# An S5 state-space layer and a SwiGLU layer summed on one NeuronCore: rotations batched over pairs of quarters, and an order chosen among 72 plans

## The chip, the core and the metric

The kernel runs on one core of a Trainium2 chip. The metric is the device time of one execution in microseconds (us), as the median of several runs. The engines named below are PE (TensorE, matrix products and transposes into PSUM), DVE (VectorE), ACT (ScalarE), POOL (GpSimd) and SP (SyncE, here only a queue for DMA). Each engine works through its own list of instructions in order, and lists meet only at semaphores.

## What is computed

`x` has 2048 rows of 512. All of it is bf16 at the edges. With `xn` the layer norm of `x` over its 512 columns, the output is `x` plus an S5 layer of `xn` plus a SwiGLU layer of `xn`:

```python
Lam_bar = exp(dt * Lam)                        # 512 complex states
Bu = xn @ B_bar.T                              # complex
h[t] = Lam_bar * h[t-1] + Bu[t]                # over the 2048 rows
yA = 2 * real(h @ C.T) + xn * Dskip
yB = (silu(xn @ w_gate) * (xn @ w_up)) @ w_down   # 512 -> 1376 -> 512
out = x + yA + yB
```

## The kernel before, in words

The rows are cut into four blocks (b = 0 to 3) of 512 rows, each of four tiles of 128 rows. The hidden width 1376 is cut into 11 pieces (f = 0 to 10; the last has 96 columns). The 512 states are cut into four quarters q of 128, each with a real and an imaginary part c.

For each block the work is this, with lines of the kernel before:

- Layer norm statistics (L513, L515 on ACT, or L541, L556 on DVE), the normalised rows `xn` (L576 POOL, L579 and L584 ACT, L586 DVE), four transposes per tile into the PSUM tiles `pT` (L601, two of them in turn) and their copies into `xnT` (L606, L613 on ACT; L609, L614 on DVE). In block 0 the chain per tile is: statistics, a logarithm and an exponential on ACT (L545, L547), one small product on DVE (L549, called nmr below), then `xn` (even tiles on POOL, odd ones on ACT).
- Gate and up products: for each f, four matmuls `G_f` and four matmuls `U_f` over 512 rows (L780, in block 0 for f = 0 and 1 in pieces of 128 rows, L789), into four PSUM tiles `pA` used in turn. ACT takes `G_f` through SiLU (L799). In blocks 0 and 1 DVE multiplies the up product in PSUM with it (L807); in blocks 2 and 3 ACT copies it first (L802) and DVE multiplies in SBUF (L804). The product is `hT_f`.
- `S_in`: 8 groups of four matmuls (L755) make `Bu`, and ACT or DVE (L761, L762) copies each group to `U`.
- `ssm_chain`: a rotation by a table of cosines and sines turns the complex recurrence into two real ones. Per quarter: two products with the tables (L826 `ri_P`, L828 `ri_Q`), their sum (L830 `ri_V`), two scans with a real decay (L839), two products back (L842 `ro_P`, L844 `ro_Q`) and their difference (L846 `ro_H`), all on DVE. P, Q and V exist twice (`qs = q % 2`), so that two quarters can be under way at a time. The last column of each block, rotated (L853 to L859), starts the next.
- `DO`: per tile of 128 rows one PSUM tile `pACC` (two in turn) sums 8 matmuls of `H` with `CT` (L879), four with the diagonal of `Dskip` (L882) and 11 of `hT` with `wd` (L892). DVE adds `x` (L898, called final below), and SP stores the tile (L900).

Once only: transposes of B (L704, 4 sets of 8) with copies into `BT` (L708 DVE, L709 ACT); transposes of C (L722, 4 sets of 8, called CTr below), which ACT and DVE scale into `CT` (L729, L734 on ACT, L731, L736 on DVE); the tables (L678 to L691; the cosine table `c512` is the last one, L691 on ACT); and 12 matmuls on zeros at the start (L472).

The order of instructions is not that of the text. `add` records each operation with what it reads and writes, its engine (some may go to ACT or DVE, whichever is free) and an assumed duration, and `schedule` (L95) plans. `_backward` gives each operation a latest start from the planned PE order and a correction `boost`; this is its priority. `_forward` then simulates the engines: among the operations that are ready within `LOOK` = 450 ns the one of earliest priority goes next, and if that would leave a hole, a ready one that fits the hole goes before it. This is done three times. `emit` (L269) writes each engine's list with its waits. SP's DMAs all have one priority and go in the order of the text.

Of the kernel before, what the change touches and what calls it, by code (L numbers as in the profile page):

```python
# [2 lines left out]

# [10 lines left out]
_SYNC_LAT = 90.0  # L14
_DMA_LAT = 1900.0
_DMA_NS_PER_BYTE = 1.0 / 330.0
# [12 lines left out]
class _Prog:  # L29
# [65 lines left out]
    def schedule(self, iters=3):  # L95
        ops = self.ops
        n = len(ops)
        for op in ops:
            op.succ = []
        for op in ops:  # L100
            for d in op.deps | op.odeps:
                ops[d].succ.append(op.idx)
        t = self.pe_t0
        anchors = {}
        for op in ops:
            if op.eng == "pe":
                anchors[op.idx] = t
                t += op.dur
        for it in range(iters):
            self._backward(anchors)  # L110
            self._forward()
            prev = -1e15
            for op in ops:
                if op.eng == "pe":
                    v = op.start
                    if v < prev:
                        v = prev
                    anchors[op.idx] = v
                    prev = v
        return self.order  # L120

    def _backward(self, anchors):
        ops = self.ops
        n = len(ops)
        t_end = max(anchors[i] + ops[i].dur for i in anchors) + 3000.0
        big = 1e15
        ls = [None] * n
        nsucc = [len(op.succ) for op in ops]
        lf = [t_end] * n
        free_before = {}  # L130
        avail = []
        for op in ops:
            if nsucc[op.idx] == 0:
                avail.append(op.idx)
        placed = 0
        while avail:
            bi = 0
            bk = (lf[avail[0]], avail[0])
            for j in range(1, len(avail)):
                kk = (lf[avail[j]], avail[j])  # L140
                if kk > bk:
                    bk = kk
                    bi = j
            i = avail[bi]
            avail[bi] = avail[-1]
            avail.pop()
            op = ops[i]
            if i in anchors:
                s_ = anchors[i]
            else:  # L150
                e_ = min(lf[i], free_before.get(op.eng, big))
                occ = op.dur + (op.nbytes * _DMA_NS_PER_BYTE if op.dma else 0.0)
                s_ = e_ - occ
                free_before[op.eng] = s_
            ls[i] = s_
            placed += 1
            for d in op.deps | op.odeps:
                dop = ops[d]
                lat = 0.0 if d in op.odeps else _SYNC_LAT
                if dop.dma:  # L160
                    lat += _DMA_LAT
                v = s_ - lat
                if v < lf[d]:
                    lf[d] = v
                nsucc[d] -= 1
                if nsucc[d] == 0:
                    avail.append(d)
        assert placed == n
        for op in ops:
            if op.eng == "sp":  # L170
                op.prio = (0.0, op.idx)
            else:
                op.prio = (ls[op.idx] + op.boost, op.idx)

    def _forward(self):
        ops = self.ops
        n = len(ops)
# [6 lines left out]
        free_at = {e: 0.0 for e in engs}  # L184
        ready = {e: [] for e in engs}
        order = {e: [] for e in engs}
# [15 lines left out]
                push_ready(op.idx)  # L202
        dma_free = 0.0
        nsched = 0
        LOOK = 450.0

        def dur_on(i, e):
            o = ops[i]
# [2 lines left out]
        while nsched < n:  # L211
            best = None
            for e in engs:
                rl = ready[e]
                if not rl:
                    continue
                tmin = min(ops[i].ready for i in rl)
                t = max(free_at[e], tmin)
                cand = [i for i in rl if ops[i].ready <= t + LOOK]
                c = min(cand, key=lambda i: ops[i].prio)  # L220
                if ops[c].ready > t:
                    hole = ops[c].ready - t
                    fit = [i for i in rl if ops[i].ready <= t and dur_on(i, e) <= hole + 20.0]
                    if fit:
                        c = min(fit, key=lambda i: ops[i].prio)
                st = max(free_at[e], ops[c].ready)
                key = (st, st + dur_on(c, e))
                if best is None or key < best[0]:
                    best = (key, e, c)
            assert best is not None, "scheduler deadlock"  # L230
            (st, _k), e, c = best
            op = ops[c]
# [9 lines left out]
            if op.dma:  # L242
# [3 lines left out]
                else:  # L246
                    xs = max(issue_end, dma_free)
                    xe = xs + op.nbytes * _DMA_NS_PER_BYTE
                    dma_free = xe
# [6 lines left out]
            for s in op.succ:  # L256
                sop = ops[s]
                sop.nrem -= 1
                if c in sop.odeps:
                    r = (op.start + op.dur) if op.dma else op.end  # L260
                else:
                    r = op.end + _SYNC_LAT
# [66 lines left out]
def _d_dve(n, mode=1, naps=0, base=70.0):  # L329
    return base + 1.04 * n / mode + 60.0 * naps  # L330
# [7 lines left out]
def bass_parallel_sum__ssm_conv_s5__swiglu_ffn__prompt_kernel(  # L338
# [8 lines left out]
    add = pg.add  # L347
    add_flex = pg.add_flex

    with ExitStack() as es:  # L350
# [22 lines left out]
        hT = sb("hT", [128, 2, 11, 512], BF16)  # L373
        U = sb("U", [128, 2, 4, 2, 512], BF16)
        PQV = sb("PQV", [128, 3, 2, 2, 512], BF16)
        Pt = PQV[:, 0, :, :, :]
        Qt = PQV[:, 1, :, :, :]
        Vt = PQV[:, 2, :, :, :]
        G = sb("G", [128, 4, 2, 512], BF16)
        NH = 2  # L380
        H = sb("H", [128, NH, 4, 2, 512], BF16)
# [11 lines left out]
        YscK = [("H", 0, q) for q in range(4)]  # L393
        UscK = [("H", 1, q) for q in range(4)]
        RscK = [("G", q, c) for q in range(4) for c in range(2)]
        AscK = [("P", 0), ("P", 1), ("Q", 0), ("Q", 1)]
        c512 = sb("c512", [128, 4, 512], BF16)
        ssT = sb("ssT", [128, 4, 2, 512], BF16)
        NO = 3
# [12 lines left out]
        st = sb("st", [128, 8, 16], F32)  # L412
        pexp = sb("pexp", [128, 16], F32)
        init = sb("init", [128, 4, 2], F32)
# [56 lines left out]
        for w_ in range(NWARM):  # L471
# [8 lines left out]
            writes=["io_i"], dur=1000, name="iota")  # L480
# [329 lines left out]
        def ssm_chain(b, pr):  # L810
            rr, S5, C5 = pr["rr"], pr["S5"], pr["C5"]
            hb = b % NH
            ub = b % 2
            for q in range(4):
                qs = q % 2
                Uq = U[:, ub, q, :, :]
                Usw = bass.AP(U[:].tensor, Uq.offset + 512, [list(Uq.ap[0]), [-512, 2], [1, 512]])
                cc = c512[:, q, :].unsqueeze(1).to_broadcast([128, 2, 512])
                ss = ssT[:, q, :, :]
                Pq, Qq, Vq, Gq = Pt[:, qs, :, :], Qt[:, qs, :, :], Vt[:, qs, :, :], G[:, q, :, :]  # L820
                Gsw = bass.AP(G[:].tensor, Gq.offset + 512, [list(Gq.ap[0]), [-512, 2], [1, 512]])
                tabs = ["tab_s", "tab_ns", "tab_c"]
                uk = [("U", ub, q, 0), ("U", ub, q, 1)]
                gk = [("G", q, 0), ("G", q, 1)]
                d2 = _d_dve(1024, 2)
                add("dve", lambda e, Pq=Pq, Uq=Uq, cc=cc: e.tensor_tensor(Pq, Uq, cc, ALU.mult),  # L826
                    reads=uk + tabs, writes=[("P", qs)], dur=d2, name="ri_P")
                add("dve", lambda e, Qq=Qq, Usw=Usw, ss=ss: e.tensor_tensor(Qq, Usw, ss, ALU.mult),  # L828
                    reads=uk + tabs, writes=[("Q", qs)], dur=d2, name="ri_Q")
                add("dve", lambda e, Vq=Vq, Pq=Pq, Qq=Qq: e.tensor_tensor(Vq, Pq, Qq, ALU.add),  # L830
                    reads=[("P", qs), ("Q", qs)], writes=[("V", qs)], dur=d2, name="ri_V")
                for c in range(2):
                    if b == 0:
                        ini = 0.0
                        ir = []
                    else:
                        ini = init[:, q, c:c + 1]
                        ir = [("init", c)]
                    add("dve", lambda e, q=q, c=c, qs=qs, ini=ini: e.tensor_tensor_scan(  # L839
                            G[:, q, c, :], rr[0][:, q:q + 1].to_broadcast([128, 512]), Vt[:, qs, c, :], ini, ALU.mult, ALU.add),  # L840
                        reads=[("V", qs), rr[1]] + ir, writes=[("G", q, c)], dur=_d_dve(512, 0.5, 1, 75), name="scan")
                add("dve", lambda e, Pq=Pq, Gq=Gq, cc=cc: e.tensor_tensor(Pq, Gq, cc, ALU.mult),  # L842
                    reads=gk + tabs, writes=[("P", qs)], dur=d2, name="ro_P")
                add("dve", lambda e, Qq=Qq, Gsw=Gsw, ss=ss: e.tensor_tensor(Qq, Gsw, ss, ALU.mult),  # L844
                    reads=gk + tabs, writes=[("Q", qs)], dur=d2, name="ro_Q")
                add("dve", lambda e, q=q, Pq=Pq, Qq=Qq: e.tensor_tensor(H[:, hb, q, :, :], Pq, Qq, ALU.subtract),  # L846
                    reads=[("P", qs), ("Q", qs)], writes=[("H", hb, q)], dur=d2, name="ro_H")
            if b < NB - 1:
                a4 = G[:, :, 0, 511]
                b4 = G[:, :, 1, 511]  # L850
# [152 lines left out]
```

## Time and profile before

| What | us |
|---|---|
| median of 6 runs | 198.11 |
| lowest, highest run | 197.97, 198.95 |
| the profiled execution, its own time | 198.85 |
| its span, first to last instruction | 197.1 |
| time outside of the span (198.85 - 197.1) | 1.75 |
| PE busy | 188.3 |
| DVE busy | 161.3 |
| ACT busy | 93.2 |

The six runs were 198.18, 197.97, 198.04, 198.95, 198.75 and 197.99. A row of the timeline reads: start, duration, engine, line, operation, what it writes and reads, count, and in brackets the idle time before it with what ended it. The chain of waits, read in order of time, gives start, duration and line of the work that ended last, each step being what released the next.

### The profile page before, as it was taken

Reading aid. Unit: us, or ns where it says so; the run is one execution under the profiler, and the core shown is the slowest. Engines: PE = TensorE matmul, PEld = TensorE weight load, DVE = VectorE, ACT = ScalarE, POOL = GpSimd, SP = SyncE. Lnnn points to the kernel's source line nnn. Section 1 sums busy time; section 2 is a strip of 40 time slices with the busy share of each in tenths; the row PEclk is TensorE's granted clock in tenths of the full one; section 3 lists DMA queues with packets and bytes.
Section 4 is the critical chain, followed back from the end, with each engine's and each line's share of the span. In section 5 each row is a group of like instructions: output and inputs, shape, how many; then the busy total and the mean of one; then the engine's idle time right before and its main releaser. Section 6 shows DMA issues by size and latency. Waiting matters only on the chain.

```text
span 197.1 us, 2753 instructions
## 1 busy us (share of the span) xinstructions
PE 188.3 (96%) x1037; PEld 93.1 (47%) x1037; DVE 161.3 (82%) x306; ACT 93.2 (47%) x174; POOL 6.3 (3%) x13
## 2 busy tenths in 40 slices
PE   7698999979999979999999999999999999999993
PEld 2495444444455544454444454445444454444541
DVE  5779894679889999999999999989999999931111
ACT  3758586987777788550046643700266502100000
POOL 2300100020000000200000000000000000000000
PEclk9879999999999999999999999999999999999999
DMA  5999960000000000000000010000000000000110
GB/s 136 319 360 360 349 190 5 0 0 0 0 3 0 0 0 0 5 27 27 0 0 3 0 45 10 27 3 27 0 0 0 27 30 28 27 27 30 41 39 27
DMA packets 11197, 10.70 MB, mean 54 GB/s; under 512 B 592, under 2 KB 11184, under 8 KB 11184
## 3 DMA queue, kind: packets, MB, share of 16 engines
q1 hardware_dynamic: 11152, 10.52, 16.7%
q8 instruction: 8, 0.13, 0.3%
q14 instruction: 5, 0.04, 0.1%
q10 hardware_dynamic: 32, 0.00, 0.0%
HBM read 8.43 MB, written 2.10 MB: 53 GB/s over the span
## 4 chain that ended last, share of the span: by engine, by line
PE 87%; DVE 6%; ACT 2%; DMA 1%; issue 1%; POOL 0%; SPq 0%; DVEq 0%; ACTq 0%
PE pA L780 32%; PE pACC L892 19%; PE pA L755 14%; PE pACC L879 14%; PE pA L789 2%; PE pACC L882 2%; PE pT L601 2%; DMA xnat<-in_A_x_dram 1%; ACT xnT L613 1%; PE pT L722 1%; DVE bnst L541 1%; PE pT L704 1%; DVE ostage L898 1%; DVE PQV L826 1%; DVE PQV L844 1%; DVE PQV L828 1%
## 5 line engine op out<-in xcount | busy, mean ns | idle before, releaser
L799 ACT ACTIVATE sg<-pA 128x512 bf16<-128x512 f32 (+1 forms) x44 | 26.2, 596 | 52.1 <-PE pA L780 36.0
L780 PE MATMUL pA<-xnT,wu 128*128 128x512 bf16 (+1 forms) x168 | 43.1, 379 | 0.0
L780 PE MATMUL pA<-xnT,wg 128*128 128x512 bf16 (+1 forms) x168 | 43.1, 379 | 0.0
L892 PE MATMUL pACC<-wd,hT 128*128 128x512 bf16 (+1 forms) x176 | 40.6, 379 | 0.0
L879 PE MATMUL pACC<-CT,H 128*128 128x512 bf16 x128 | 30.3, 379 | 0.1
L755 PE MATMUL pA<-xnT,BT 128*128 128x512 bf16 x128 | 28.3, 379 | 1.7 <-ACT xnT L613 1.1
L839 DVE TENSOR_TENSOR_SCAN G<-sm,init,PQV 128x512 bf16<-128x512 f32 x24 | 29.9, 1273 | 0.0
L898 DVE TENSOR_TENSOR ostage<-pACC,xnat 128x512 bf16<-128x512 f32 x16 | 11.0, 688 | 19.2 <-PE pACC L892 19.1
L780 PEld LDWEIGHTS pA<-xnT,wg 128*128 128x128 bf16 (+1 forms) x168 | 16.7, 100 | 19.1
L780 PEld LDWEIGHTS pA<-xnT,wu 128*128 128x128 bf16 (+1 forms) x168 | 16.6, 100 | 18.7 <-DVE hT L807 0.4
L892 PEld LDWEIGHTS pACC<-wd,hT 128*128 128x128 bf16 (+1 forms) x176 | 16.5, 98 | 17.0
L755 PEld LDWEIGHTS pA<-xnT,BT 128*128 128x128 bf16 x128 | 12.4, 98 | 16.6 <-ACT xnT L613 2.0
L879 PEld LDWEIGHTS pACC<-CT,H 128*128 128x128 bf16 x128 | 12.4, 98 | 15.2 <-DVE ostage L898 0.2
L761 ACT ACTIVATE U<-pA 128x512 bf16<-128x512 f32 x25 | 14.7, 597 | 8.9 <-PE pA L755 8.7
L807 DVE TENSOR_TENSOR hT<-pA,sg 128x512 bf16<-128x512 f32 (+1 forms) x22 | 15.0, 686 | 4.4 <-PE pA L780 2.7
L802 ACT ACTIVATE su<-pA 128x512 bf16<-128x512 f32 (+1 forms) x22 | 13.1, 596 | 5.3 <-PE pA L780 5.3
L828 DVE TENSOR_TENSOR PQV<-U,ssT 128x1024 bf16<-128x1024 bf16 x16 | 11.0, 688 | 0.0
L826 DVE TENSOR_TENSOR PQV<-U,c 128x1024 bf16<-128x1024 bf16 x16 | 11.0, 687 | 0.0
L844 DVE TENSOR_TENSOR PQV<-G,ssT 128x1024 bf16<-128x1024 bf16 x16 | 11.0, 686 | 0.0
L842 DVE TENSOR_TENSOR PQV<-G,c 128x1024 bf16<-128x1024 bf16 x16 | 10.9, 681 | 0.0
L830 DVE TENSOR_TENSOR PQV<-PQV 128x1024 bf16<-128x1024 bf16 x16 | 10.7, 687 | 0.0
L846 DVE TENSOR_TENSOR H<-PQV 128x1024 bf16<-128x1024 bf16 x16 | 10.5, 686 | 0.0
(94 smaller groups left out, 159.1 us busy)
## 6 DMA issues: line engine op xcount, KB each, us to landing
out_dram<-ostage SPq DMA_DIRECT2D x16, 128.0 KB, 1.7
xnat<-in_A_x_dram SPq DMA_DIRECT2D x3, 512.0 KB, 9.3
wd<-in_B_w_down_dram SPq DMA_DIRECT2D x1, 1280.0 KB, 11.8
xnat<-in_A_x_dram SPq DMA_DIRECT2D x4, 128.0 KB, 2.4
wg<-in_B_w_gate_dram SPq DMA_DIRECT2D x1, 512.0 KB, 6.1
wu<-in_B_w_up_dram SPq DMA_DIRECT2D x1, 512.0 KB, 7.0
U<-in_A_B_re_dram SPq DMA_DIRECT2D x1, 512.0 KB, 8.0
U<-in_A_B_im_dram SPq DMA_DIRECT2D x1, 512.0 KB, 8.9
```

Source lines behind the costliest of these rows:

```text
L755: ins = e.matmul(pA[bank][:, :], BT[:, k, c * 512 + 128 * q:c * 512 + 128 * (q + 1)], xnT[:, b, k, :], start=(k == 0), stop=(k == 3))
L761: ("act", lambda e, q=q, c=c, bank=bank: e.activation(U[:, b % 2, q, c, :], pA[bank][:, :], AF.Copy), _d_act(512, True)),
L780: ins = e.matmul(pA[bank][0:fs, :], w[:, k, f0:f0 + fs], xnT[:, b, k, :], start=(k == 0), stop=(k == 3))
L799: add("act", lambda e: e.activation(sg[0:fs, slot, :], pA[bg][0:fs, :], AF.Silu), reads=[("pA", bg), "@t1"], writes=[("sg", slot)], dur=_d ...
L802: add("act", lambda e: e.activation(su[0:fs, slot, :], pA[bu][0:fs, :], AF.Copy), reads=[("pA", bu)], writes=[("su", slot)], dur=_d_act(51 ...
L807: add("dve", lambda e: e.tensor_tensor(hT[0:fs, b % 2, f, :], pA[bu][0:fs, :], sg[0:fs, slot, :], ALU.mult), reads=[("sg", slot)], writes= ...
L826: add("dve", lambda e, Pq=Pq, Uq=Uq, cc=cc: e.tensor_tensor(Pq, Uq, cc, ALU.mult), reads=uk + tabs, writes=[("P", qs)], dur=d2, name="ri_P")
L828: add("dve", lambda e, Qq=Qq, Usw=Usw, ss=ss: e.tensor_tensor(Qq, Usw, ss, ALU.mult), reads=uk + tabs, writes=[("Q", qs)], dur=d2, name="r ...
L839: add("dve", lambda e, q=q, c=c, qs=qs, ini=ini: e.tensor_tensor_scan(G[:, q, c, :], rr[0][:, q:q + 1].to_broadcast([128, 512]), Vt[:, qs, ...
L844: add("dve", lambda e, Qq=Qq, Gsw=Gsw, ss=ss: e.tensor_tensor(Qq, Gsw, ss, ALU.mult), reads=gk + tabs, writes=[("Q", qs)], dur=d2, name="r ...
L879: ins = e.matmul(pACC[bank][:, :], H[:, hb, q, c, tsl], CT[:, c * 4 + q, :], start=first, stop=False)
L892: ins = e.matmul(pACC[bank][:, :], hT[0:fs, hs, f, tsl], wd[0:fs, f, :], start=False, stop=(f == NF - 1))
```

## The change

Two things are changed. First, `ssm_chain` works on pairs of quarters: each of the six rotation operations covers 2048 elements per partition in place of 1024, and there is one P, one Q and one V in place of two half-sized ones. The 8 scans per block stay as they are. Second, `schedule` plans 72 times, over three values of the look-ahead (60, 250, 450), the hole rule on or off, random noise of several sizes on the priorities, and `boost` at full size or times 0.7. `_replay` walks each plan with exact durations and again with durations 6% longer (PE's excepted) and later releases; the plan with the least mean of the two is used. The one it settles on has a look-ahead of 60, the hole rule, noise of up to 200 with seed 2, and `boost` times 0.7. All other operations are those of before.

```diff
+        cands = []
+        for look in (60.0, 250.0, 450.0):
+            for hole in (True, False):
+                for sigma, seed in ((0.0, 0), (200.0, 1), (200.0, 2), (500.0, 3), (500.0, 4), (900.0, 5)):
+                    for bs in (1.0, 0.7):
+                        cands.append(dict(look=look, hole=hole, sigma=sigma, seed=seed, bscale=bs, iters=iters))
...
+        for p in cands:
+            self._sched_once(p)
+            nom = self._replay(1.0, 0.0)
+            pert = self._replay(1.06, 60.0)
+            score = 0.5 * nom + 0.5 * pert
...
+        self._sched_once(best[1])
...
+    def _sched_once(self, p):
...
+        rs = np.random.RandomState(p["seed"])
+        self._noise = rs.uniform(-1.0, 1.0, size=n) * p["sigma"]
+        self._bscale = p["bscale"]
+        self._look = p["look"]
+        self._hole = p["hole"]
...
+    def _replay(self, scale, lat_add):
...
+                    st = max(free_at[e], r)
+                    dur = op.dur * (scale if e != "pe" else 1.0)
...
-                op.prio = (ls[op.idx] + op.boost, op.idx)
+                op.prio = (ls[op.idx] + op.boost * self._bscale + self._noise[op.idx], op.idx)
...
-        LOOK = 450.0
+        LOOK = self._look
...
-                if ops[c].ready > t:
+                if self._hole and ops[c].ready > t:
...
-            for q in range(4):
-                qs = q % 2
...
-                d2 = _d_dve(1024, 2)
-                add("dve", lambda e, Pq=Pq, Uq=Uq, cc=cc: e.tensor_tensor(Pq, Uq, cc, ALU.mult),
-                    reads=uk + tabs, writes=[("P", qs)], dur=d2, name="ri_P")
...
+            d4 = _d_dve(2048, 2)
+            Pp, Qp, Vp = PQV[:, 0, :, :, :], PQV[:, 1, :, :, :], PQV[:, 2, :, :, :]
+            for pp in range(2):
+                q0 = 2 * pp
+                Up = U[:, ub, q0:q0 + 2, :, :]
+                Usw = bass.AP(U[:].tensor, Up.offset + 512, [pst, [1024, 2], [-512, 2], [1, 512]])
+                cc = c512[:, q0:q0 + 2, :].unsqueeze(2).to_broadcast([128, 2, 2, 512])
+                ss = ssT[:, q0:q0 + 2, :, :]
...
+                add("dve", lambda e, Up=Up, cc=cc: e.tensor_tensor(Pp, Up, cc, ALU.mult),
+                    reads=uk + tabs, writes=[("P",)], dur=d4, name="ri_P")
+                add("dve", lambda e, Usw=Usw, ss=ss: e.tensor_tensor(Qp, Usw, ss, ALU.mult),
+                    reads=uk + tabs, writes=[("Q",)], dur=d4, name="ri_Q")
+                add("dve", lambda e: e.tensor_tensor(Vp, Pp, Qp, ALU.add),
+                    reads=[("P",), ("Q",)], writes=[("V",)], dur=d4, name="ri_V")
...
+                add("dve", lambda e, Gp=Gp, cc=cc: e.tensor_tensor(Pp, Gp, cc, ALU.mult),
+                    reads=gk + tabs, writes=[("P",)], dur=d4, name="ro_P")
+                add("dve", lambda e, Gsw=Gsw, ss=ss: e.tensor_tensor(Qp, Gsw, ss, ALU.mult),
+                    reads=gk + tabs, writes=[("Q",)], dur=d4, name="ro_Q")
+                add("dve", lambda e, q0=q0: e.tensor_tensor(H[:, hb, q0:q0 + 2, :, :], Pp, Qp, ALU.subtract),
+                    reads=[("P",), ("Q",)], writes=[("H", hb, q0), ("H", hb, q0 + 1)], dur=d4, name="ro_H")
```

Built, the two kernels hold the same PE, ACT and SP work in other places, and DVE 48 rotation instructions in place of 96. Where PE's list is rearranged:

| Place | before | after |
|---|---|---|
| first gate and up pieces | transposes of tiles 0, 1, 2, then G and U in turn | transposes 0, 1, one G piece, transpose 2, three U pieces, ... |
| B transposes | one run of 32 between G_2 and U_2 | 16 after G_3 and G_2; U_2, U_3; then 16 |
| first C transposes | in block 1, after f = 4 | 8 of them between the row transposes of block 1 and its S_in |
| row transposes of block 2 | 8, U_10, 8 | U_10, then 16 |
| DO of block 0 | after G_0, U_0, G_1, U_1 of block 2 | after G_0 of block 2 |

On DVE and ACT the copies of `U` are shared differently, and DVE's chain of block 0 begins inside the first S_in. From G_2 of block 2 on PE's list is that of before.

More of the change, by code (lines that the diff above doesn't have):

```diff
@@ L1 @@
 import math
+import numpy as np
 from contextlib import ExitStack
@@ L102, in schedule @@
                 ops[d].succ.append(op.idx)
+        cands = []
[4 more added lines that the diff above has]
+                        cands.append(dict(look=look, hole=hole, sigma=sigma, seed=seed, bscale=bs, iters=iters))
+        best = None
+        self.trace = []
+        for p in cands:
[3 more added lines that the diff above has]
+            score = 0.5 * nom + 0.5 * pert
+            self.trace.append((score, nom, pert, p))
+            if best is None or score < best[0]:
+                best = (score, p)
+        self._sched_once(best[1])
+        self.best = best
+        return self.order
+    def _sched_once(self, p):
+        ops = self.ops
+        n = len(ops)
+        for op in ops:
+            if op.alts:
+                e0 = None
+                for e in op.alts:
+                    e0 = e
+                    break
+                op.eng = e0
+                op.fn, op.dur = op.alts[e0]
+        rs = np.random.RandomState(p["seed"])
[3 more added lines that the diff above has]
+        self._hole = p["hole"]
         t = self.pe_t0
@@ L108, in schedule @@
                 t += op.dur
-        for it in range(iters):
+        for it in range(p["iters"]):
             self._backward(anchors)
@@ L119, in schedule @@
                     prev = v
-        return self.order
+    def _replay(self, scale, lat_add):
+        ops = self.ops
+        order = self.order
+        ptr = {e: 0 for e in order}
+        free_at = {e: 0.0 for e in order}
+        end = {}
+        issue = {}
+        dma_free = 0.0
+        remaining = sum(len(v) for v in order.values())
+        mk = 0.0
+        while remaining:
+            progressed = False
+            for e, lst in order.items():
+                while ptr[e] < len(lst):
+                    i = lst[ptr[e]]
+                    op = ops[i]
+                    r = 0.0
+                    ok = True
+                    for d in op.deps:
+                        if d not in end:
+                            ok = False
+                            break
+                        v = end[d] + _SYNC_LAT + lat_add
+                        if v > r:
+                            r = v
+                    if ok:
+                        for d in op.odeps:
+                            if d not in end:
+                                ok = False
+                                break
+                            v = issue[d]
+                            if v > r:
+                                r = v
+                    if not ok:
+                        break
+                    st = max(free_at[e], r)
+                    dur = op.dur * (scale if e != "pe" else 1.0)
+                    if op.dma:
+                        ie = st + op.dur
+                        if op.nbytes < 65536:
+                            en = ie + op.nbytes * _DMA_NS_PER_BYTE + _DMA_LAT + 4 * lat_add
+                        else:
+                            xs = max(ie, dma_free)
+                            xe = xs + op.nbytes * _DMA_NS_PER_BYTE * scale
+                            dma_free = xe
+                            en = xe + _DMA_LAT + 4 * lat_add
+                        free_at[e] = ie
+                        issue[i] = ie
+                    else:
+                        en = st + dur
+                        free_at[e] = en
+                        issue[i] = en
+                    end[i] = en
+                    if en > mk:
+                        mk = en
+                    ptr[e] += 1
+                    remaining -= 1
+                    progressed = True
+            assert progressed, "replay deadlock"
+        return mk
@@ L375, in bass_parallel_sum__ssm_conv_s5__swiglu_ffn__prompt_kernel @@
         PQV = sb("PQV", [128, 3, 2, 2, 512], BF16)
-        Pt = PQV[:, 0, :, :, :]
-        Qt = PQV[:, 1, :, :, :]
-        Vt = PQV[:, 2, :, :, :]
         G = sb("G", [128, 4, 2, 512], BF16)
@@ L395, in bass_parallel_sum__ssm_conv_s5__swiglu_ffn__prompt_kernel @@
         RscK = [("G", q, c) for q in range(4) for c in range(2)]
-        AscK = [("P", 0), ("P", 1), ("Q", 0), ("Q", 1)]
+        AscK = [("P",), ("Q",)]
         c512 = sb("c512", [128, 4, 512], BF16)
@@ L813, in ssm_chain @@
             ub = b % 2
-            for q in range(4):
-                qs = q % 2
[L816 to L824, printed above, removed]
-                d2 = _d_dve(1024, 2)
-                add("dve", lambda e, Pq=Pq, Uq=Uq, cc=cc: e.tensor_tensor(Pq, Uq, cc, ALU.mult),
-                    reads=uk + tabs, writes=[("P", qs)], dur=d2, name="ri_P")
[L828 to L847, printed above, removed]
@@ new lines, in ssm_chain @@
+            pst = list(U[:].ap[0])
+            gst = list(G[:].ap[0])
+            tabs = ["tab_s", "tab_ns", "tab_c"]
+            d4 = _d_dve(2048, 2)
[6 more added lines that the diff above has]
+                ss = ssT[:, q0:q0 + 2, :, :]
+                Gp = G[:, q0:q0 + 2, :, :]
+                Gsw = bass.AP(G[:].tensor, Gp.offset + 512, [gst, [1024, 2], [-512, 2], [1, 512]])
+                uk = [("U", ub, q, c) for q in (q0, q0 + 1) for c in range(2)]
+                gk = [("G", q, c) for q in (q0, q0 + 1) for c in range(2)]
+                add("dve", lambda e, Up=Up, cc=cc: e.tensor_tensor(Pp, Up, cc, ALU.mult),
[4 more added lines that the diff above has]
+                    reads=[("P",), ("Q",)], writes=[("V",)], dur=d4, name="ri_V")
+                for qi in range(2):
+                    q = q0 + qi
+                    for c in range(2):
+                        if b == 0:
+                            ini = 0.0
+                            ir = []
+                        else:
+                            ini = init[:, q, c:c + 1]
+                            ir = [("init", c)]
+                        add("dve", lambda e, q=q, c=c, qi=qi, ini=ini: e.tensor_tensor_scan(
+                                G[:, q, c, :], rr[0][:, q:q + 1].to_broadcast([128, 512]), Vp[:, qi, c, :], ini, ALU.mult, ALU.add),
+                            reads=[("V",), rr[1]] + ir, writes=[("G", q, c)], dur=_d_dve(512, 0.5, 1, 75), name="scan")
+                add("dve", lambda e, Gp=Gp, cc=cc: e.tensor_tensor(Pp, Gp, cc, ALU.mult),
[4 more added lines that the diff above has]
+                    reads=[("P",), ("Q",)], writes=[("H", hb, q0), ("H", hb, q0 + 1)], dur=d4, name="ro_H")
```

## The prediction, as it was put on record

> **What bounds the kernel.** I read the engines' shares first, then PE's waits, then the chain of waits in order of time, and then timelines of the places that these name. The shares:
>
> ```profile
> PE 188.3 (96%) x1037; PEld 93.1 (47%) x1037; DVE 161.3 (82%) x306; ACT 93.2 (47%) x174; POOL 6.3 (3%) x13
> ```
>
> PE is busy for 188.3 of 197.1 us and the change leaves its matmuls alone, so only PE's holes and its slow stretches can be won. Four matmuls over 512 rows start every 0.8635 us (78.57, 79.44, 80.30, 81.16 in PE's timeline), a transpose every 0.055 us (0.44 for 8). PE's own waits, largest among them:
>
> ```profile
> PE pT L601 <- POOL xn L576: 1.1, 1, 1.1
> PE pA L755 <- ACT xnT L613: 1.1, 1, 1.1
> PE pA L755 <- DVE xnT L614: 0.6, 1, 0.6
> ```
>
> The first is the wait for the first normalised rows. The others, and one that is split over several rows, are places where PE transposes and then waits for the copies out of two PSUM tiles. The chain of waits shows three such places (start, duration, work):
>
> ```profile
> 15.08 0.91 PE pT L704 x16
> ...
> 16.01 1.03 ACT BT L709
> ...
> 17.09 0.62 PE pT L704 x8
> ...
> 39.41 0.46 PE pT L601 x8
> ...
> 41.04 0.44 DVE xnT L614
> ...
> 41.61 7.07 PE pA L755 x32
> ...
> 69.06 1.08 ACT xnT L613 x2
> ...
> 71.66 7.08 PE pA L755 x32
> ```
>
> From 71.66 to 194.02 the chain is PE without a hole worth naming. One more loss lies in the granted clock (columns: stretch, length, PE busy, clock, DMA):
>
> ```profile
> 5.00:8.50 3.50, 1.84 (x15) 1.00 1.03 301
> 8.50:12.00 3.50, 3.50 (x36) 0.51 1.08 374
> ```
>
> After 3.5 us with PE half idle, PE ran at half clock for 3.5 us.
>
> **Cost of the change on DVE.** 96 rotation instructions become 48. The rows say 687 ns each, but back to back they start 0.60 apart, since the end of one overlaps the next. Dependent neighbours do not overlap:
>
> ```profile
> 10.81 0.17 DVE L499 TENSOR_SCALAR sm<-sm 128x4 f32<-128x4 f32 x1
> 11.02 0.17 DVE L500 TENSOR_SCALAR sm<-sm 128x4 f32<-128x4 f32 x1
> ...
> 43.35 0.69 DVE L826 TENSOR_TENSOR PQV<-U,c 128x1024 bf16<-128x1024 bf16 x1
> 43.95 0.69 DVE L828 TENSOR_TENSOR PQV<-U,ssT 128x1024 bf16<-128x1024 bf16 x1
> ```
>
> [...] L499 to L500, where the second reads the first, start 0.21 apart, against 0.07 for independent small ones (112.77 and 112.84): a dependent neighbour costs 0.13. Before, two quarters alternated and hid this. In the built order of the new kernel six rotation steps directly follow what they read (0.13 each) and about eight have one tiny instruction between (0.06 each): 1.3 us. [...]
>
> **PE's places, one by one.** I walked the new lists of PE, ACT and DVE by hand, with durations of the rows (ACT copy 0.5 start to start, B copy 0.95, table step 1.8 to 2.0; DVE copy or hT from PSUM 0.60, scan 1.19).
>
> Head, +0.3. Tile 2's nmr, before at 6.3, now stands on DVE behind the parameter products and three L673, in the slot of tile 3's (8.23). POOL follows 0.35 later: `xn` of tile 2 at 9.3, transpose at 9.35 in place of 8.41. One G piece fills 0.43 of that; PE idles 0.5 more, and of this half is recovered because less work is left in the slow stretch. The G and U pieces end at about 14.37, not 14.05.
>
> B transposes, -0.87. Before: 14.91 to 17.54 for 32 x 0.055 = 1.76, so 0.87 lost on copies. Now G_3 and G_2 go first, the 16 transposes come at 16.1, U_2 and U_3 (1.73) cover two ACT copies (16.7 to 18.65), and the second 16 start at 18.7. U_5 then needs hT_3, which DVE reaches after the table step L683 and four L556 at about 21.4, against PE's arrival at 22.2: no wait. What if the cover is gone: up to 0.87 is back. U_10 ends at 31.75 (before 32.34).
>
> Between S_in of blocks 0 and 1, -0.07. Before 9.27 us from start to start; 6.91 are matmuls. Now the copies of the row transposes wait for DVE's second rotation and an ACT statistic, giving 9.2 us, but 8 C transposes (0.44) lie inside this hole and leave block 1.
>
> Block 1, -0.75. Before, from S_in to S_in 30.05 us. Now 6.91 + 22 x 0.8635 + 24 x 0.055 + 2.0 = 29.2; the 2.0 are 16 row transposes with their copies, now after U_10. Before the same piece, with U_10 inside it, took 2.86, that is 2.0 beside it: nothing is won there. The gain is the 0.44 moved and 0.23 of waits between C transposes, and about 0.1 of small ones. [...]
>
> DO of block 0, 0. It now starts one group after S_in, 7.8 us after that began. H must be ready: DVE's chain begins about 7.4 us earlier than before (the cosine table comes at 35.7, not 43.3, as ACT does it after one copy of `U`), carries six more copies of `U`, and ends 7.1 us after the start of S_in. Slack 0.7 us; before it was 0.3 (81.75 against 82.03).
>
> From there on the places are those of before, DVE is early, and the chain of block 3 is done some 12 us before its DO. Tail, stores and the 1.75 us outside the span are untouched. The new planner's search is done before launch and costs the chip nothing.
>
> Sum: +0.3 - 0.87 - 0.07 - 0.75 = -1.4 us. From the profiled 198.85 this gives 197.45; the median of 6 runs is 0.74 lower, so with the same difference 196.7.
>
> **Bounds.** Head: the late tile costs 0.2 to 0.6. [...] Taking the row's lesson that partly idle counts, the half clock could last one more window, in which PE does half the work: at most +1.7. At 16 to 18 the trace has 1.54 busy of 2 and keeps full clock, so I take 0, being nearer. The other waits: each of the four places can be wrong by about 0.3 either way; the largest gain, if all the holes named went, is 0.87 + 0.52 + 0.61 + 0.23 + 1.1 = 3.3, less the moved loads. The gain in an undisturbed clock is larger by up to 0.5, since PE then no longer stands before the B load.
>
> **Rivals.** (1) Hidden anyway: PE is at its floor and the new holes replace the old; then 198.1. For it: PE's 96%, and the late tile 2. Against: the holes at 15 and 57 have cover in the new order. (2) Half clock for a second window: -1.4 + 1.7 = +0.3, 198.4. It shares its result with (1). (3) Slower: DO of block 0 waits for H. If a dependent 2048-element operation waited longer than 0.13, the twelve rotations of block 0 would make H late, and every microsecond beyond the slack of 0.7 is PE idle, with nothing else in its list. [...] At 0.3 each it gives 3.6 - 0.7 - 1.4 = +1.5, 199.6. Against: dependent small ones lose 0.13, and fillers stand between most. [...]
>
> **How the numbers follow.** Forecast 0.70, its own range 195.8 to 197.5. Rivals (1) and (2) together 0.2, (3) 0.1. A difference of 0.3%, 0.6 us, is about what can be told from none. Faster: nearly all of the forecast and a little of the first rivals, 0.71; same 0.18; slower 0.11. The range is 195.7 to 198.3: it leaves out (3), and gains above 2.4.
>
> **What would show it.** Right: rotations of 2048 at 1.22 us, starting 1.13 apart; `xn` of tile 2 at 8.5 or later; B transposes in two runs of 16 with no hole between 16 and 23; S_in of block 1 at about 41, S_in of block 2 near 70.2 and DO of block 0 at 78, without a wait on H. Wrong: half clock after 12.5, a PE wait on L946, or hT waits in the first gate and up stage that eat the 0.87.

## The result, and the profile after

| What (us) | before | after |
|---|---|---|
| median | 198.21 (20 runs) | 196.16 (10 runs) |
| lowest, highest run | 197.75, 198.95 | 195.9, 198.0 |
| the profiled execution, its own time | 198.85 | 196.35 |
| its span | 197.1 | 194.6 |
| PE busy | 188.3 | 187.2 |
| DVE busy | 161.3 | 158.9 |

The ratio is 0.9923 with an interval of 0.9898 to 0.9948: faster by 0.5 to 1.0%, or about 1.5 us (2.05 by the medians). The forecast was 196.7. The page of the changed kernel, first the shares and then the costliest DVE group:

```profile
PE 187.2 (96%) x1037; PEld 91.7 (47%) x1037; DVE 158.9 (82%) x259; ACT 92.6 (48%) x173; POOL 7.3 (4%) x13
...
L924 DVE TENSOR_TENSOR PQV<-U,c 128x2048 bf16<-128x2048 bf16 x8 | 9.8, 1223 | 0.2
```

A rotation over 2048 elements takes 1.22 us. PE's waits after, without one of 1.2 on L567 at the start that both kernels have:

```profile
PE pT L696 <- POOL xn L671: 0.9, 2, 0.6
PE pA L850 <- DVE xnT L709: 0.6, 1, 0.6
PE pA L884 <- ACT xnT L701: 0.5, 1, 0.5
PE pT L696 <- ACT xnT L708: 0.5, 1, 0.5
```

The wait of 1.1 before S_in of block 2 (`pA` from the copy L613) is gone. In its place are two, 0.5 for a copy by ACT (L708) and 0.6 for one by DVE (L709), as all 16 row transposes now stand after U_10. The chain of waits in order of time (start, duration, work) shows what lies in the former holes:

```profile
9.20 0.40 PE pT L696 x4
...
13.17 1.73 PE pA L875 x8
14.89 0.89 PE pT L799 x16
15.79 1.73 PE pA L875 x8
17.51 0.89 PE pT L799 x16
18.41 12.18 PE pA L875 x56
...
38.68 0.61 ACT xnT L708
39.28 0.05 issue
39.33 0.62 PE pT L817 x8
39.95 6.95 PE pA L850 x32
...
68.80 0.44 DVE xnT L709
69.24 0.08 issue
69.32 7.07 PE pA L850 x32
76.38 0.86 PE pA L875 x4
77.25 1.73 PE pACC L979 x8
```

The two runs of B transposes (L799) stand between gate and up groups without a hole, eight C transposes (L817) stand ahead of the S_in of block 1, and DO of block 0 (L979) follows one group after the S_in of block 2, without a wait. A row of the chain starts when the work before it has ended; in PE's timeline a row starts when its first matmul does, some 0.17 earlier in a row without holes. So DO of block 0 is at 77.25 here and at 77.08 in the timeline. Places below are those of the timeline.

One caution on the pair of profiles. The profile before has the half-clock stretch at 8.5 to 12 us and the one after has not; here PE was busy for 2.67 of 3.5 us in the window ahead of it (stretch, length, PE busy, clock, DMA):

```profile
5.00:8.50 3.50, 2.67 (x17) 1.00 1.02 297
```

The order does not decide it alone. Of the 11 executions of the changed kernel, 7 ran at a mean granted clock of 0.997 or more (median 196.09) and 4 at 0.991 (median 197.77); the profile was one of the 7. The profile before, at 0.989, was the rarer case: of 41 later executions of that kernel, 6 were at 0.991 or less. For accounts I therefore use e5 and e6 below, both kernels at full clock throughout.

### The profile page after: what moved, and what is told of

Its sections match the earlier page's. It is cut to its first block, busy times and chain, and to the rows that moved or that the text cites. A ratio compares the mean times of both kernels' runs of the same rounds, so it can differ in the third digit from the quotient of the medians.

```text
span 194.6 us, 2700 instructions
## 1 busy us (share of the span) xinstructions
PE 187.2 (96%) x1037; PEld 91.7 (47%) x1037; DVE 158.9 (82%) x259; ACT 92.6 (48%) x173; POOL 7.3 (4%) x13
## 4 chain that ended last, share of the span: by engine, by line
PE 91%; DVE 4%; DMA 1%; ACT 1%; POOL 1%; issue 0%; SPq 0%; DVEq 0%
PE pA L875 37%; PE pACC L992 20%; PE pACC L979 14%; PE pA L850 13%; PE pACC L982 2%; PE pA L884 2%; PE pT L696 2%; DMA xnat<-in_A_x_dram 1%; PE pT L817 1%; DVE bnst L636 1%; PE pT L799 1%; POOL xn L671 1%; DVE U L857 1%; ACT xnT L708 1%; DVE PQV L926 1%; DVE PQV L924 0%
## 5 line engine op out<-in xcount | busy, mean ns | idle before, releaser
L875 PE MATMUL pA<-xnT,wu 128*128 128x512 bf16 (+1 forms) x168 | 42.5, 379 | 0.0
L875 PE MATMUL pA<-xnT,wg 128*128 128x512 bf16 (+1 forms) x168 | 42.5, 379 | 0.0
L979 PE MATMUL pACC<-CT,H 128*128 128x512 bf16 x128 | 30.2, 379 | 0.0
L939 DVE TENSOR_TENSOR_SCAN G<-sm,init,PQV 128x512 bf16<-128x512 f32 x24 | 29.4, 1271 | 0.0
L850 PE MATMUL pA<-xnT,BT 128*128 128x512 bf16 x128 | 28.3, 379 | 0.6 <-DVE xnT L709 0.6
L850 PEld LDWEIGHTS pA<-xnT,BT 128*128 128x128 bf16 x128 | 12.4, 98 | 15.4 <-DVE xnT L709 0.7
L979 PEld LDWEIGHTS pACC<-CT,H 128*128 128x128 bf16 x128 | 12.5, 98 | 14.9
L856 ACT ACTIVATE U<-pA 128x512 bf16<-128x512 f32 x23 | 13.7, 596 | 8.8 <-PE pA L850 8.7
L924 DVE TENSOR_TENSOR PQV<-U,c 128x2048 bf16<-128x2048 bf16 x8 | 9.8, 1223 | 0.2
L946 DVE TENSOR_TENSOR H<-PQV 128x2048 bf16<-128x2048 bf16 x8 | 9.8, 1222 | 0.0
L942 DVE TENSOR_TENSOR PQV<-G,c 128x2048 bf16<-128x2048 bf16 x8 | 9.8, 1221 | 0.0
L944 DVE TENSOR_TENSOR PQV<-G,ssT 128x2048 bf16<-128x2048 bf16 x8 | 9.8, 1220 | 0.0
L928 DVE TENSOR_TENSOR PQV<-PQV 128x2048 bf16<-128x2048 bf16 x8 | 9.8, 1220 | 0.0
L926 DVE TENSOR_TENSOR PQV<-U,ssT 128x2048 bf16<-128x2048 bf16 x8 | 9.8, 1219 | 0.0
```

Source lines behind the costliest of these rows:

```text
L850: ins = e.matmul(pA[bank][:, :], BT[:, k, c * 512 + 128 * q:c * 512 + 128 * (q + 1)], xnT[:, b, k, :], start=(k == 0), stop=(k == 3))
L856: ("act", lambda e, q=q, c=c, bank=bank: e.activation(U[:, b % 2, q, c, :], pA[bank][:, :], AF.Copy), _d_act(512, True)),
L875: ins = e.matmul(pA[bank][0:fs, :], w[:, k, f0:f0 + fs], xnT[:, b, k, :], start=(k == 0), stop=(k == 3))
L924: add("dve", lambda e, Up=Up, cc=cc: e.tensor_tensor(Pp, Up, cc, ALU.mult), reads=uk + tabs, writes=[("P",)], dur=d4, name="ri_P")
L926: add("dve", lambda e, Usw=Usw, ss=ss: e.tensor_tensor(Qp, Usw, ss, ALU.mult), reads=uk + tabs, writes=[("Q",)], dur=d4, name="ri_Q")
L939: add("dve", lambda e, q=q, c=c, qi=qi, ini=ini: e.tensor_tensor_scan(G[:, q, c, :], rr[0][:, q:q + 1].to_broadcast([128, 512]), Vp[:, qi, ...
```

## The experiments

Each starts from one of the two kernels. `place(eng, op, after)` moves one operation in an engine's finished list. The intervals of the ratios are against the kernel before.

**e1 and e2: each half of the change alone.** e1 is the `ssm_chain` of before under the new `schedule`; e2 is the new `ssm_chain` under the old `schedule`.

```diff
 e1
-    def schedule(self): (one plan)
+    def schedule(self): (72 plans, _sched_once, _replay)
 e2
-            for q in range(4):            (96 rotations)
+            for pp in range(2):           (48 rotations)
```

> The rotations of before (96 of 1024), planned with the new search, which here settles on noise of up to 500 with seed 4. Theory (the order of PE's list makes the gain): as the changed kernel or nearly, ratio to before 0.990 to 0.995, since this list too splits the B transposes and puts 8 C transposes before the second S_in. Rival (the time that the paired rotations take from DVE makes it): 1.00, 198.2 us.

> The paired rotations with the planner of before (look-ahead 450, no noise). Its list keeps the B transposes in one run of 32. Theory (order): ratio 0.997 to 1.003, the B transposes lose about 0.85 us as before. Rival (DVE's saving): 0.990 to 0.995, about 196.5 us.

e1: 196.81, ratio 0.9925 (0.9913 to 0.9938). e2: 203.33, ratio 1.0243 (1.0225 to 1.0261). The search alone gives most of the gain, although it settles on another plan (noise up to 500, look-ahead 60). At full clock e1 has 196.80 and the kernel before, in the same set of runs, 198.29: 1.5 us, where e3 below, with the order of the changed kernel, has 2.2 (196.05). What is missing lies in the head: S_in of block 0 starts at 31.03, in e3 at 30.24, and PE waits 1.0 for the load of B. Pairing alone costs 5 us, which no theory had. PE's waits in e2 are headed by this row:

```profile
PE pT L598 <- DVE CT L733: 1.9, 1, 1.9
```

and DVE's timeline there shows what PE waits behind:

```profile
68.06 1.22 DVE L826 TENSOR_TENSOR PQV<-U,c 128x2048 bf16<-128x2048 bf16 x1
69.20 1.22 DVE L828 TENSOR_TENSOR PQV<-U,ssT 128x2048 bf16<-128x2048 bf16 x1
70.33 0.74 DVE L733 SCALAR_TENSOR_TENSOR CT<-pT,sm,ctmp 128x512 bf16<-128x512 bf16 x1
```

The last scaling of C (L733) reads one of the two `pT` tiles, and the row transposes of block 2 need that tile. The old planner puts two rotations, now 2.26 us in one piece, ahead of it. What follows is in the windows (stretch, length, busy and count of PE, PEld, DVE, ACT and POOL, then clock, DMA, GB/s):

```profile
66.00:74.00 8.00, 4.01 (x28) 2.12 (x28) 8.00 (x10) 6.74 (x17) 0.00 (x0) 0.85 0.00 0
74.00:78.00 4.00, 4.00 (x10) 1.44 (x10) 4.00 (x6) 1.19 (x2) 0.00 (x0) 0.50 0.00 0
```

PE is idle for half of 8 us, and then runs at half clock. From the S_in of block 1 to that of block 2 e2 takes 33.49 us, the kernel before 30.05, and the S_in of block 2 itself takes 8.9 in place of 6.9. Two of the five executions of e2 had the clock of this profile (0.982; 203.60 and 203.74), three a higher one (0.992; 202.66 to 203.33).

**e3 and e9: the order held, the rotations cut.** e3 keeps every list of the changed kernel and issues each of the six rotations as two of 1024 elements (e9: as four of 512).

```diff
-  e.tensor_tensor(Pp, Up, cc, ALU.mult)
+  for h in range(2):
+      ins = e.tensor_tensor(Pp[:, h, :, :], Up[:, h, :, :], cc[:, h, :, :], ALU.mult)
```

> The changed kernel with every list in its order, but each paired rotation issued as two of 1024 elements one after the other: DVE does 48 more instructions, some 3.2 us. Theory (order): the time of the changed kernel within 0.3 us, as PE has 0.84 us in hand at the DO of block 0 (H ends at 76.24, DO starts at 77.08) and 12 more issues cost 0.8. Rival (DVE's saving): 2 to 3 us slower than the changed kernel, the time of before.

> The changed kernel with every list in its order, but each paired rotation issued as four of 512 elements: DVE gets 144 more instructions, some 9.6 us, of which 12 x 3 x 0.067 = 2.4 us lie before H of block 0 is done. Theory (PE's slack at that DO is 0.84 us and nothing else in PE's list covers it): DO of block 0 waits about 1.5 us, and the later hT and finals add little; 197 to 199 us. Rival (DVE is far from PE's path everywhere): 196.1.

Both expectations take 0.067 us for an added instruction, an estimate. By starts, a rotation of 2048 elements takes 1.13 in one piece (after, 86.55 to 87.68), 1.21 in two (e3, 72.34 to 73.55) and 1.35 in four (e9, 74.43 to 75.78): 0.07 to 0.08 for each added instruction.

e3: 196.06, ratio 0.9898 (0.987 to 0.9926), that of the changed kernel (0.9923). With the order fixed, the fewer instructions are worth nothing that can be measured. e9: 200.62, ratio 1.0143 (1.0098 to 1.0187), above the 197 to 199 of the theory. DVE does begin to bind when it gets more fixed cost, but not where I had said. DO of block 0 starts at 78.90 and `H` is done at 78.67: still 0.23 to spare. PE waits at the row transposes and the end tiles instead:

```profile
PE pT L696 <- DVE xnT L709: 2.2, 2, 1.6
PE pACC L985 <- DVE ostage L1004: 1.8, 1, 1.8
```

The wait of 1.6 ends at 118.45, ahead of the S_in of block 3, and the one of 1.8 at 170.80, at an end tile. From the S_in of block 1 to the end of `H` e9 took 37.0 us, the changed kernel 36.43. DVE was busy for 36.76 and 35.27 of these, so it did 1.49 more in 0.57 more time: its own waits took up most of the load. The profiled execution of e9 (202.26) had the half clock as well. In it a first window with 2.40 of 3.5 us busy was followed by half clock, and its first B transpose came 1.64 later than in e3, whose lists are the same. The other three executions ran at 0.997 or more and took 200.54 to 200.63, so the 4.5 us that the median lies above the changed kernel are not clock.

**e4: the B transposes in one run again.** The changed kernel, with all 32 after G_3 and G_2, and U_2 and U_3 behind them.

```diff
+  place("pe", find("pe", "BTr", 2), find("pe", "BTr", 1))
+  place("pe", find("pe", "BTr", 3), find("pe", "BTr", 2))
```

> The changed kernel with PE's list altered in one place: the 32 B transposes in one run after G_3 and G_2, U_2 and U_3 after them. Theory (order, with cover of the copies by U_2 and U_3 worth 0.87): 0.8 to 0.9 us slower than the changed kernel, with PE waits on the B copies of that sum. Rival (the clock alone makes the difference of the two kernels): no difference beyond noise.

197.31, ratio 0.9975 (0.9951 to 1.0). Among executions at a clock of 0.997 or more it is 197.27 against 196.09: +1.2, where 0.8 to 0.9 was expected. S_in of block 0 starts at 31.59, not 30.43. PE's waits name the copies, and PE's timeline shows where:

```profile
PE pT L799 <- ACT BT L804: 1.0, 2, 0.7
...
14.35 1.05 PE L799 MATMUL pT<-ident,U 128*128 128x128 bf16 x16
16.10 0.62 PE L799 MATMUL pT<-ident,U 128*128 128x128 bf16 x8 [0.70 <-ACT BT L804]
17.01 0.62 PE L799 MATMUL pT<-ident,U 128*128 128x128 bf16 x8 [0.30 <-ACT BT L804]
17.47 1.89 PE L875 MATMUL pA<-xnT,wu 128*128 128x512 bf16 x8
```

The waits of 1.0 count from the end of the last matmul; in a row without holes the next one starts some 0.17 before that end. By starts, the 32 transposes take 3.12 us (14.35 to 17.47) for 1.76 of work: 1.36 lost. Before it was 0.87. There DVE made the first copy that PE waits for (0.69 us); here ACT makes both (1.02 each). S_in of block 0 comes 1.35 later than in e3, and 0.12 of it comes back before the S_in of block 1. So this one cover, taken out of the new order, costs more than half of the gain.

**e5 and e6: both kernels at full clock.** A few matmuls on zeros (6 in e5, 8 in e6) go into early holes of PE; their results are not used.

```diff
+  def warm(i, n): op i also issues n matmuls on zeros into pACC[1]
+  warm(last, 4); warm(tt_[1], 2)
+  warm(pe[nm.index("Gt")], 2)        (e6 only)
```

> The kernel before with six more matmuls on zeros, four after the last one at the start and two after the second row transposes, so that PE has no hole of half a microsecond between 6 and 8.5; their result is not used. Theory (the half clock at 8.5 to 12 comes from those holes and costs this kernel little, since PE then waits for the B load): no run with a granted clock under 0.997, time 198.0 to 198.4, ratio 0.997 to 1.000. Rival (the half clock is most of what separates the two kernels): 197 or less.

> The changed kernel with eight more matmuls on zeros in its three holes between 6 and 9.2 (four, two, two); their result is not used. Theory: the runs near 197.5 to 198.0 with clock 0.991 disappear and all are at 195.9 to 196.4. Rival (clock drops come whatever PE does): the share of such runs stays at a third.

e5: 197.97, ratio 0.999 (0.9976 to 1.0004). e6: 196.12, ratio 0.9896 (0.9883 to 0.9909). None of their 16 executions had a clock below 0.998, where the changed kernel had 4 of 11 at 0.991. The kernel before gains little by it, for two reasons. Its median of 198.13 in the same set of runs is already one of full clock (15 of 17 executions; the two others took 198.77 and 199.06). And this row appears among PE's waits in e5:

```profile
PE pT L704 <- DMA U<-in_A_B_im_dram: 0.5, 1, 0.5
```

PE arrives earlier and stands before the load of B. The half clock delayed the first B transpose by only 0.97 (13.94 in e5, 14.91 in the profile before). The changed kernel has one more group ahead of the B transposes and reaches them at 14.53 (e6), without such a wait, so it loses more by the half clock: 1.7 (197.77 against 196.09). With the clock out of the way the two differ by 1.85.

**e7 and e8: the late tile 2 mended.** e7 is the changed kernel with the exponentials and nmr products of tiles 2 and 3 moved ahead of what the search had put before them. e8 adds six of the matmuls on zeros.

```diff
+  place("act", find("act", "ln_exp", 2), find("act", "ln_ln", 2))
+  place("act", find("act", "ln_exp", 3), find("act", "ln_ln", 3))
+  place("dve", n3, n2); place("dve", n2, find("dve", "prm32", 0))
```

> The changed kernel with two places of the head altered: on ACT the exponential of tiles 2 and 3 right after their logarithm, on DVE the small product of tile 2 right after the copy of the parameters and that of tile 3 in its old slot. Theory (the late tile 2 costs the head 0.3): third row transposes at about 8.3 instead of 9.2, PE's wait of 0.57 there gone, 0.3 to 0.5 us faster than the changed kernel. Rival (the head waits for something else anyway): no change.

> Both alterations, with six matmuls on zeros (four, two). Theory: sum of the two, 195.6 to 195.9 with no run of low clock, faster than both kernels. Rival: the zeros delay the rows that matter and eat the gain, 196.1.

e7: 195.88, ratio 0.9886 (0.9872 to 0.9899). e8: 195.68, ratio 0.9878 (0.9863 to 0.9892), the best of all. The third transposes come at 8.14 in place of 9.20, but a new wait of 0.28 for a copy (L704) follows, and S_in of block 0 starts 0.4 to 0.6 earlier (29.81 against 30.23 in e6 and 30.43). In time it is 0.2 (195.88 against 196.09) to 0.4 (195.68 against 196.12), less than the 0.3 to 0.5 expected of e7; the intervals of e6, e7 and e8 overlap, so the size is not firm.

**e10: the loss of e2 mended.** e2 with the last C scaling ahead of the two rotations on DVE, and the last two row-transpose copies ahead of five statistics on ACT.

```diff
+  before("dve", cw, hm)
+  before("act", tev[2], st1)
+  before("act", tev[3], st1)
```

> The paired rotations in the old planner's order (203.3 us), with two things moved: on DVE the last scaling of C goes ahead of the two rotations that stand before it, on ACT the last two copies of the row transposes of block 2 go ahead of five statistics. Theory (that paired rotation, 2.26 us in one piece, holds the PSUM tile that the row transposes need, and the hole of some 4 us behind it costs PE its clock for 3.4 us more): the hole and the half clock go, S_in of block 2 takes 6.9 us, 4 to 5.5 us faster, 198 to 199.5. Rival (pairing costs DVE time that shows elsewhere): 201 or more.

200.95, ratio 1.0136 (1.0108 to 1.0164). By the ratios, 2.1 of e2's 4.8 us come back; the theory had 4 to 5.5, and the result lies almost at the rival's 201. The half-clock stretch is gone (clock 1.00 from 60 to 80) and the S_in of block 2 is 31.05 after that of block 1. Two new waits take part of it:

```profile
PE pACC L881 <- DVE H L848: 0.8, 1, 0.8
PE pA L752 <- DVE hT L804: 0.7, 1, 0.7
```

The first is the prediction's third rival, at its place, in an order that leaves `H` no slack. DVE's total load does not explain it: it is busy for 157.5 us here and 161.3 before. Against e5, PE ends 3.4 us later in this profile: 0.7 before the S_in of block 0 (PE waits 1.2 for the load of B, in e5 0.5), 1.0 between the S_in of blocks 1 and 2, and 2.0 after that, where the two rows lie; 0.3 is gained between the S_in of blocks 0 and 1. So the two places named for e2 are about half of what pairing costs in the old order. Of the rest, 1.5 is PE waiting for DVE in the two rows.

## Why the prediction was right

The theory was that the gain lies in PE's order and not in DVE's lighter load. e1 and e3 show this, and e4 shows which piece of the order holds most of it. The number itself was met with some luck, as the last points show. The starts of S_in at full clock, in e5 (L755) and e6 (L850):

```profile
31.37 7.07 PE L755 MATMUL pA<-xnT,BT 128*128 128x512 bf16 x32
40.63 7.07 PE L755 MATMUL pA<-xnT,BT 128*128 128x512 bf16 x32 [0.61 <-DVE xnT L614]
70.68 7.08 PE L755 MATMUL pA<-xnT,BT 128*128 128x512 bf16 x32 [1.05 <-ACT xnT L613]
119.35 7.07 PE L755 MATMUL pA<-xnT,BT 128*128 128x512 bf16 x32
...
30.23 7.07 PE L850 MATMUL pA<-xnT,BT 128*128 128x512 bf16 x32
39.61 7.08 PE L850 MATMUL pA<-xnT,BT 128*128 128x512 bf16 x32
69.11 7.07 PE L850 MATMUL pA<-xnT,BT 128*128 128x512 bf16 x32 [0.56 <-DVE xnT L709]
117.55 7.07 PE L850 MATMUL pA<-xnT,BT 128*128 128x512 bf16 x32
```

The time between them, in us:

| Piece | e5 (before) | e6 (after) | difference | predicted |
|---|---|---|---|---|
| start to S_in of block 0 | 31.37 | 30.23 | -1.14 | +0.3 - 0.87 = -0.57 |
| S_in of block 0 to block 1 | 9.26 | 9.38 | +0.12 | -0.07 |
| block 1 to block 2 | 30.05 | 29.50 | -0.55 | -0.75 |
| block 2 to block 3 | 48.67 | 48.44 | -0.23 | 0 |
| S_in of block 3 to the end of PE | 73.68 | 73.67 | 0 | 0 |
| sum | | | -1.80 | -1.4 |

- **Head, +0.3.** Tile 2's transposes came at 9.20 (predicted 9.35). Mending the lateness is worth 0.2 to 0.4 (e7, e8), about the size predicted.
- **B transposes, -0.87.** From the first of them to S_in is 17.43 in e5 with 17 groups behind them. Less one group of 0.8635 that is 16.57, and e6 takes 15.70: -0.87 as predicted. Taking the cover away costs 1.2 rather than "up to 0.87" (e4), since PE then waits for two copies by ACT. With the head's +0.3 that makes -0.57; the table has 0.57 more, about as much as e5's hole before the load of B: 0.46 in the row of waits, 0.62 by starts. The prediction named this as a possible gain in an undisturbed clock, outside of its sum.
- **Between S_in of blocks 0 and 1, -0.07.** It was +0.12: the eight C transposes lie in the hole, after an ACT copy at 38.68, and the hole is a little longer than I had walked.
- **Block 1, -0.75.** It was -0.55. (The prediction's own 30.05 and 29.2 would give -0.85; the -0.75 is its list of gains, 0.44, 0.23 and 0.1.) The step that was off is "the 2.0 are 16 row transposes with their copies". By starts they took from 67.06 to 69.32 after, 2.26 us, with waits of 0.47 for ACT and 0.56 for DVE. In part this was misread before: the 2.86 came from the chain, whose row starts at 68.80, but PE's timeline has

```profile
68.64 0.61 PE L601 MATMUL pT<-ident,xn 128*128 128x128 bf16 x8
```

  and so 3.02 to the S_in at 71.66, 2.16 without U_10. With 2.16 the working gives -0.66. The row transposes became 0.1 longer instead of staying as they were, and that is the rest.
- **DO of block 0, 0, with a slack of 0.7.** `H` ended at 76.24 and DO began at 77.08: slack 0.84 and no wait. That rotations of 2048 elements would start 1.13 apart was an estimate that no row of before shows; it held after. The rival's price was also near: dependent rotations start 1.26 apart, independent ones 1.13 to 1.14, so a dependent neighbour costs 0.13, as taken from the small operations. DVE's and PE's timelines after:

```profile
75.02 1.22 DVE L946 TENSOR_TENSOR H<-PQV 128x2048 bf16<-128x2048 bf16 x1
77.08 1.89 PE L979 MATMUL pACC<-CT,H 128*128 128x512 bf16 x8
...
87.68 1.22 DVE L944 TENSOR_TENSOR PQV<-G,ssT 128x2048 bf16<-128x2048 bf16 x1
88.94 1.23 DVE L946 TENSOR_TENSOR H<-PQV 128x2048 bf16<-128x2048 bf16 x1
```

- **DVE.** Busy time fell by 2.4 (161.3 to 158.9), beside PE's work. In it are two more copies of `U` on DVE (9 in place of 7, and ACT 23 in place of 25) and one `xn` fewer, 0.9 us at the paces of the rows; so the rotations saved about 3.3, an estimate. At the 0.07 to 0.08 an instruction of e3 and e9, 48 fewer make 3.4 to 3.8. e9 shows where this cost binds: at the row transposes (a wait of 1.6) and end tiles (1.8), and not at DO of block 0, as the third rival had it.
- **"From there on the places are those of before", 0.** It was -0.23. Before, the DO of block 1 waited 0.2 for a final (L898): from the row transposes ahead of it 0.66 by starts (114.88 to 115.54), in e6 0.45. This wait is gone, and I had not listed it.
- **The clock.** I took a second half-clock window as the risk, and none was seen. What I missed is that the first one need not occur: at a given order it comes in some executions only (4 of 11 after). The prediction carried the profile's stretch over to both kernels. On that premise S_in of block 0 would start some 1.65 later than in e6 (e9 against e3 shows 1.64), at 31.9 against 32.34 before, which is -0.44 where -0.57 was predicted. The rows below it stay as in the table, and the sum is -1.1, not -1.4. The medians of the executions with the stretch agree roughly: 197.77 after, 198.6 to 198.9 before. In the other 7 of 11 executions the change is worth about 2 (1.8 in the table), in part since PE then no longer stands before the B load. The step from 197.45 to 196.7 has the same flaw. The 0.74 between the profiled execution and the median was carried over as a fixed difference, but it is probably for the most part what the half clock costs the kernel before (0.3 in the set run with e1, 0.8 in the one with e5), and the same stretch costs the changed kernel 1.7. So the predicted 196.7 is met partly by luck, because the two errors have opposite signs: the terms were 0.3 too favourable, and the clock was better than assumed.

What stays open: what decides in which executions the half clock comes, and what costs e10 the 1.0 between the S_in of blocks 1 and 2. Putting U_10 back between the two halves of block 2's row transposes was not tried in the new order.

## What to carry to other kernels

When one engine is busy for 96% and the edit lightens another, price the order and not the load: list the bounded engine's holes one by one and ask which work the new order puts into each. Longer pieces on a helper engine save fixed cost (here 0.07 to 0.08 us an instruction) but delay the small hand-offs behind them (in e2 PE waited 1.9 us for one), and an order planned for short pieces can lose far more than the saving (5 us here). Before comparing two profiles, look whether the granted clock was the same in both, and in how many executions.

## What was not expected of the hardware

- **The half clock came after windows that were only partly idle, and their idle share did not foretell it.** In the first window, PE busy for 1.84 (before) and 2.40 (e9) of 3.5 us was followed by half clock; 2.67 (after), 3.13 (e5) and 3.34 (e8) kept full clock. But so did 2.05 (e7) and 2.08 (e10), and the least busy one of all, that of e1 (stretch, length, PE busy, clock, DMA):

```profile
5.00:8.50 3.50, 1.54 (x16) 1.00 1.04 309
8.50:12.00 3.50, 3.50 (x66) 1.00 1.09 376
```

  The two that lost the clock were not idle, and these traces give no threshold. What they show is that it varies from execution to execution of one kernel: a mean clock of 0.991 or less in 6 of 41 later executions of the kernel before and in 4 of 11 of the changed one.
- **A few matmuls on zeros may prevent it.** None of the 16 executions of e5 and e6 had the stretch, and the zeros cost nothing measurable (196.12 against 196.09 for the full-clock executions of the changed kernel). Without them it came in 2 of 17 executions of the kernel before, in the same set of runs, and in 4 of 11 of the changed kernel. e8 had none in 4, but neither had e7, without zeros. The counts are small, so this is likely and not proven.
